# Windowed attention and a squared-ReLU FFN on one core: the first query and key chunks loaded two tokens to a partition and turned by ordinary matmuls, value blocks loaded one by one, and a new hand-written order of the head

## The chip, the cores and the metric

The kernel runs on one core of a Trainium2 chip. The metric is the device time of one execution in microseconds (us). Before the change, three runs gave 879.31, 880.03 and 880.48 us, a median of 880.03 us.

## The reference

The inputs are `q`, `k` and `v` of shape (8 batches, 8 heads, 576 tokens, 64), and the weights `w_in` (512 x 2048) and `w_out` (2048 x 512), all float32. What is computed, in short:

```python
scores = (q @ k.T) / sqrt(64)                  # per batch and head
mask = (0 <= i - j) & (i - j < 64)             # each query sees itself and the 63 keys before it
attn = softmax(where(mask, scores, -1e9))
x = (attn @ v), heads side by side             # 4608 tokens x 512
out = (max(x @ w_in, 0) ** 2) @ w_out          # 4608 x 512
```

## The kernel before, in words

**Tiles.** The 4608 tokens are cut into 12 tiles of 384 tokens (six blocks of 64). For each tile there is an attention part and an FFN part. The attention of a tile comes in three *sections* of four (block, head group) items each. Sections 0 to 2 belong to tile 0 and sections 3 to 5 to tile 1. Tile 1 crosses from batch 0 into batch 1, so sections 4 and 5 need the first 192 tokens of batch 1 as well (`FIRST`, L144).

**FFN.** Each float32 operand is split into a high and a low part, so that a product is three fast matmul passes. `mm1` (L346) makes one 128-wide slice of the hidden layer for a tile (12 matmuls of 384 columns), `evac` (L358) squares and splits it, and `mm2` (L387) accumulates it into the output (9 matmuls of 512 columns). The weights are loaded once, in 16 pieces of 1 MB (`fetch_w`, L77: one DMA for `w_in`, one for `w_out`), and each piece is split by ScalarE and VectorE in six steps (`weight`, L83). Only after all this is in place does the second half of the kernel (L541 on) run as a regular loop over tiles 2 to 11.

**The head, in a written order.** The stretch up to the regular loop has a schedule that is written out by hand: the string `order` (L475) holds one token for each step, and the engines' queues get their instructions in exactly that order. The letters that matter here:

- `L0`.. and `N0`.. load query and key chunks of batch 0 and batch 1 (`load_first`, L151); `v` loads value blocks (`load_v`, L125), `w` a weight piece. All DMAs are issued on SP's queue, in the order of the string.
- `T` and `U` turn a chunk of batch 0 and batch 1, so that the head dimension lies on the partitions (`turn_first`, L161, on TensorE into PSUM), and `t` and `u` copy the turned chunk to SBUF (`copy_first`, L172); the last letter of such a token names the engine (`a` ScalarE, `d` VectorE, `p` GpSimd).
- `S` is a section's score matmuls (L208); `o`, `s`, `z`, `y`, `e`, `f`, `k`, `R`, `m` are the masked softmax (`o` copies the scores out on ScalarE, L216; `s` puts in the masked ones on VectorE, L225 and L226; `e` and `f` are the exponentials, L236); `X` turns the probabilities (L250), `x` masks them on VectorE (L254), `V` multiplies by the values (L272); `H` and `Q` write the result's high and low part (L287, L289).
- `a b c d h l` are the six steps of a weight piece (ScalarE, VectorE three times, ScalarE, VectorE). `M`, `r p g G` and `O` are `mm1`, the evacuation and `mm2`. The first of them, `M0`, needs sections 0 to 2 and the first weight piece; in the string it stands behind section 5's scores and section 3's turn.
- `K5` is five matmuls of the identity with itself whose result nobody reads (`idle`, L497). They fill gaps of TensorE.

A chunk before is 128 tokens, one token a partition, so that one descriptor of the DMA carries the 64 floats (256 bytes) of one token and head. A turn is four PE-mode transposes (L169), one for each of (pair of heads, q or k).

Of the kernel before, what the change touches and what calls it, by code (L numbers as in the profile page):

```python
# [24 lines left out]
def window_attention_relu2_ffn(ctx: ExitStack, tc: tile.TileContext, q, k, v, w_in, w_out, out):  # L25
# [99 lines left out]
    def load_v(b, t):  # L125
        vt = vts[b, t] = att.tile([P, 2, H // 2, D], F32, name="vt", bufs=5)
        for n in range(min(2, NB - 2 * t)):
            s0 = (2 * t + n) * QB
            for m in range(2):
                sp.dma_start(vt[m * QB:(m + 1) * QB, n],  # L130
                             v[b, m * H // 2:(m + 1) * H // 2, s0:s0 + QB, :].rearrange("h s d -> s h d"))
# [11 lines left out]

    FIRST = 2 * TT - S  # L144
    nats, first = {}, {}

    def tokens(b, t):
        return min(P, (FIRST if b else S) - t * P)


    def load_first(b, t):  # L151
        n = tokens(b, t)
        if t % 2 == 0:
            both = wpool.tile([P, 2, 2, H * D], F32, name="w")
            for i in range(2):
                nats[b, t + i] = both[:, i]
        for i, x in enumerate((q, k)):
            sp.dma_start(nats[b, t][:n, i].rearrange("s (h d) -> s h d", d=D),  # L158
                         x[b, :, t * P:t * P + n, :].rearrange("h s d -> s h d"))

    def turn_first(b, t, d):  # L161
        n = tokens(b, t)
        early = b == 0 and 0 < 2 * t + d < 3
        ps = ps_o.tile([P, 2, 2, P], F32, name="oV" if early else "oT", bufs=2 if early else 1)
        if b and (t, d) == (0, 0):
            first[b] = wpool.tile([P, 2, 2, 2, FIRST], F32, name="w")
        for j in range(2):
            for i in range(2):
                pe.transpose(ps[:, j, i, :n], nats[b, t][:n, i, (2 * j + d) * P:(2 * j + d + 1) * P], ident[:n, :n])  # L169
        return ps  # L170

    def copy_first(b, t, d, ps, copy):  # L172
        n = tokens(b, t)
        qk = first[b][:, d] if b else get_turned(b, d)
        copy(qk[:, :, :, t * P:t * P + n].rearrange("p j i s -> p (j i) s"), ps.rearrange("p j i s -> p (j i) s")[:, :, :n])
# [287 lines left out]

    AHEAD, LEAD = 5, 9
    steps = [(t, f) for t in range(2) for f in range(AHEAD)]
    n0 = n1 = AHEAD
    while n1 < NF:
# [8 lines left out]
        L0 L1 w0 L2 T0 v0 T1 t0a t1d S0 w1 T2 o0a T3 K5 t2d v1 s0 t3d a0 z0 S1 L3 y0 b0 f0 N0 T4 K3 c0  # L476
        o1a L4 t4a s1 T5 K5 e0 w2 d0 t5a N1 k0 z1 h0 S2 R0 y1 v2 m0d e1 l0 X0 K6 o2a x0 a1 v3 s2 V0 f1
        b1 H0a k1 T6 K4 w3 z2 R1 y2 t6d m1p v4 f2 Q0 T7 X1 c1 t7a U0 e2 x1 S3 u0a k2 d1 V1 o3a T8 v5 H1a
        R2 s3 m2p t8a T9 a2 Q1 X2 t9d z3 h1 U2 K2 w4 b2 y3 u2a U1 K4 f3 w5 x2 u1a w6 c2 U3 e3 S4 w7 l1
        u3a V2 k3 o4a v6 R3 H2a s4 m3p Q2 S5 a3 z4 X3 o5a b3 M0 y4 f4 x3 e4 c3 V3 r0 k4 d2 p0a M1 v7 H3a  # L480
        g0 R4 Q3 m4p h2 s5 X4 r1 G0 p1a z5 O0 g1 x4 y5 e5 G1 V4 d3 f5 O1 v8 l2 H4a k5 h3 R5 Q4 m5p M2 a4
        l3 w8 w9 X5 r2 b4 a5 M3 w10 x5 p2a w11 g2 c4 r3 V5 w12 p3a G2 g3 w13 d4 O2 w14 G3 h4 H5d O3 w15
        l4 q0 Q5 a6 M4 b5 b6 r4 M5 p4a c5 g4 q1 c6 r5 M6 p5a G4 g5 d6 O4 r6 d5 h6 G5 p6a M7 h5 g6 l5 O5
        r7 G6 a7 l6 p7a O6 b7 g7 a8 G7 M8 c7 b8 O7 r8 p8a d7 g8 M9 G8 h7 c8 O8 r9 l7 p9a g9 d8 a9 M10 G9
        h8 b9 O9 r10 l8 p10a g10 c9 a10 M11 G10 b10 O10 r11 p11a d9 g11 M12 G11 h9 c10 O11 r12 l9 p12a
# [19 lines left out]
    with tc.manual_schedule(engines={E.PE, E.DVE, E.Activation, E.Pool, E.SP}):  # L505
        for token in order.split():
# [4 lines left out]
            elif op == "v":  # L511
                load_v(*divmod(n, (NB + 1) // 2))
# [76 lines left out]
```

## Time and profile before

| | us |
|---|---|
| median of three runs | 880.03 (879.31 to 880.48) |
| the profiled execution's own time | 880.19 |
| its span in the trace | 878.4 |
| TensorE busy | 860.0 of 878.4 (98%) |
| TensorE busy up to the first FFN matmul (0 to 42.59) | 30.55 of 42.59 |
| VectorE busy up to there | 28.45 of 42.59 |

The profiled execution lies 0.16 us above the median, and 1.8 us of it lie outside its span. The page has one number for each engine over the whole run; the head of the kernel, which the change edits, is the first tenth of it. It is best read with the views that take a window of time: the busy times by stretch, the chain of waits that ended last, and the timeline of a single engine. Matmuls with float32 operands appear as two rows of the trace each; transposes as one.

### The profile page before, as it was taken

Reading aid. Unit: us, or ns where it says so; the run is one execution under the profiler, and the core shown is the slowest. Engines: PE = TensorE matmul, PEld = TensorE weight load, DVE = VectorE, ACT = ScalarE, POOL = GpSimd, SP = SyncE. Lnnn points to the kernel's source line nnn. Section 1 sums busy time; section 2 is a strip of 40 time slices with the busy share of each in tenths; the row PEclk is TensorE's granted clock in tenths of the full one; section 3 lists DMA queues with packets and bytes.
Section 4 is the critical chain, followed back from the end, with each engine's and each line's share of the span. In section 5 each row is a group of like instructions: output and inputs, shape, how many; then the busy total and the mean of one; then the engine's idle time right before and its main releaser. Section 6 shows DMA issues by size and latency. Waiting matters only on the chain.

```text
span 878.4 us, 16976 instructions
## 1 busy us (share of the span) xinstructions
PE 860.0 (98%) x6946; PEld 794.7 (90%) x6946; DVE 452.0 (51%) x740; ACT 401.8 (46%) x1147; POOL 50.1 (6%) x70
## 2 busy tenths in 40 slices
PE   6799999999999999999999999999999999999998
PEld 5688998899999999999999999999999999999997
DVE  5799995754455444544455444453445544432222
ACT  5787875644344434434334444334434443432322
POOL 1210000210000000000000000000000000000000
PEclk9899999999999999999999999999999999999999
DMA  9989206460125002421033202141013200100100
GB/s 213 222 270 327 37 4 106 81 155 7 26 55 121 1 1 64 71 48 54 1 55 92 54 2 63 29 81 55 11 21 67 59 1 1 37 1 1 37 1 36
DMA packets 200302, 56.41 MB, mean 64 GB/s; under 512 B 185377, under 2 KB 193569, under 8 KB 200225
## 3 DMA queue, kind: packets, MB, share of 16 engines
q1 hardware_dynamic: 200224, 55.34, 27.4%
q8 instruction: 54, 0.88, 0.4%
q14 instruction: 24, 0.19, 0.1%
HBM read 45.88 MB, written 9.44 MB: 63 GB/s over the span
## 4 chain that ended last, share of the span: by engine, by line
PE 94%; SPq 3%; DMA 1%; ACT 1%; POOL 0%; DVE 0%; issue 0%; POOLq 0%
PE h_ps L352 42%; PE oV L396 26%; PE oT L396 14%; PE s_ps L208 3%; PE v_ps L272 3%; PE s_ps L396 2%; PE v_ps L250 1%; SPq L158 1%; PE v_ps L396 1%; SPq L130 1%; DMA w<-in_k_dram 1%; PE h_ps L500 0%; ACT sel L236 0%; SPq L80 0%; ACT r L361 0%
## 5 line engine op out<-in xcount | busy, mean ns | idle before, releaser
L352 PE MATMUL h_ps<-xhi,w 128*128 128x384 f32 x1536 | 407.0, 327 | 1.9 <-ACT r L361 1.4
L352 PEld LDWEIGHTS h_ps<-xhi,w 128*128 128x128 f32 x1536 | 275.2, 189 | 8.6 <-ACT r L361 3.3
L352 PE MATMUL h_ps<-xlo,w 128*128 128x384 f32 x768 | 250.6, 326 | 0.0
L361 ACT ACTIVATE r<-h_ps 128x384 f32<-128x384 f32 x192 | 93.6, 487 | 286.4 <-PE h_ps L352 285.7
L396 PE MATMUL oV<-w,ghi 128*128 128x512 f32 x704 | 209.5, 379 | 0.0
L366 DVE TENSOR_TENSOR r<-r 128x384 f32<-128x384 f32 x166 | 92.0, 554 | 165.4 <-ACT r L361 165.4
L371 DVE TENSOR_TENSOR glo<-r,ghi 128x384 fp32r<-128x384 f32 x192 | 107.8, 562 | 121.0 <-PE oV L396 82.0
L369 ACT CAST ghi<-r 128x384 fp32r<-128x384 f32 x192 | 98.8, 514 | 117.4 <-DVE r L366 115.4
L396 PEld LDWEIGHTS oV<-w,ghi 128*128 128x128 f32 x704 | 133.2, 189 | 18.8
L352 PEld LDWEIGHTS h_ps<-xlo,w 128*128 128x128 f32 x768 | 145.3, 189 | 4.8
L396 PE MATMUL oV<-w,glo 128*128 128x512 f32 x352 | 133.5, 379 | 0.0
L396 PE MATMUL oT<-w,ghi 128*128 128x512 f32 x352 | 110.2, 395 | 0.0
L236 ACT ACTIVATE sel<-sel,nm 128x64 f32<-128x64 f32 x272 | 90.8, 335 | 17.4 <-DVE nm L230 15.3
L396 PEld LDWEIGHTS oV<-w,glo 128*128 128x128 f32 x352 | 66.6, 189 | 9.4
L245 POOL TENSOR_TENSOR sel<-sel,rs 128x512 f32<-128x512 f32 x33 | 38.4, 1163 | 564.4 <-DVE rs L242 564.4
L396 PE MATMUL oT<-w,glo 128*128 128x512 f32 x176 | 66.8, 379 | 0.0
L254 DVE TENSOR_TENSOR pt<-v_ps,masks 128x1024 f32<-128x1024 f32 x31 | 38.0, 1224 | 46.8 <-PE v_ps L250 46.8
L396 PEld LDWEIGHTS oT<-w,ghi 128*128 128x128 f32 x352 | 59.0, 189 | 2.3 <-issue 0.2
L236 ACT ACTIVATION_READ_ACCUMULATOR sel<-sel,nm 128x1 f32 x272 | 50.9, 187 | 0.0
L140 DVE STREAM_TRANSPOSE qk<-raw 128x1152 f32<-128x1152 f32 x28 | 38.4, 1371 | 1.4 <-issue 1.4
L208 PE MATMUL s_ps<-qk 64*64 64x128 f32 (+1 forms) x1104 | 38.3, 276 | 0.1
L396 PEld LDWEIGHTS oT<-w,glo 128*128 128x128 f32 x176 | 33.3, 189 | 4.7
(80 smaller groups left out, 592.6 us busy)
## 6 DMA issues: line engine op xcount, KB each, us to landing
vt<-in_v_dram SPq DMA_DIRECT2D x144, 64.0 KB, 2.5
out_dram<-osb SPq DMA_DIRECT2D x36, 256.0 KB, 2.3
w<-in_moe_w_in_dram SPq DMA_DIRECT2D x16, 512.0 KB, 6.6
w<-in_moe_w_out_dram SPq DMA_DIRECT2D x16, 512.0 KB, 7.6
raw<-in_q_dram SPq DMA_DIRECT2D x112, 72.0 KB, 2.5
raw<-in_k_dram SPq DMA_DIRECT2D x112, 72.0 KB, 2.5
w<-in_q_dram SPq DMA_DIRECT2D x5, 256.0 KB, 4.6
w<-in_k_dram SPq DMA_DIRECT2D x5, 256.0 KB, 5.2
```

The costliest lines, as they stand in the source:

```text
L140: dve.transpose(get_turned(b, g // 2)[:, g % 2].rearrange("p n t -> p (n t)"), raw.rearrange("p n t -> p (n t)"))
L208: pe.matmul(ps[half * QB:(half + 1) * QB, j, w * P + c0:(w + 1) * P], lhsT=qk[r, 0, qb * QB:(qb + 1) * QB], rhs=qk[r, 1, k0:k0 + P - c0], ...
L236: act.activation(sels[i][:, w, hd], sels[i][:, w, hd], AF.Exp, bias=nms[i][:, n], scale=SCALE, accum_out=sums[i][:, n])
L245: (dve if eng == "d" else pool).tensor_tensor(p, p, rs[i][:, :, None].broadcast_to([P, SW * 2, QB]), ALU.mult)
L254: dve.tensor_tensor(pts[i].rearrange("p (w n) q -> p w n q", n=2), ps_t[i][:, :, None, :].broadcast_to([P, SW, 2, P]), masks.rearrange("p ...
L272: pe.matmul(ps[hd * D:(hd + 1) * D, j, q0:q0 + n * QB], lhsT=vts[b, kb // 2][r, kb % 2, 2 * d + hd, :], rhs=pts[i][r, n0:n0 + n, half * QB ...
L352: pe.matmul(h_ps, lhsT=wparts[f][:, 0, part, kk * P:(kk + 1) * P], rhs=in_turn(xx[:, kk, :]), start=n == 0, stop=n == 3 * NK - 1)
L361: act.activation(by_half(rg[n]), ordered(hs.pop(n)), AF.Relu)
L366: dve.tensor_tensor(rg[n], rg[n], rg[n], ALU.mult)
L369: act.copy(gs[n][0], rg[n])
L371: dve.tensor_tensor(gs[n][1], rg.pop(n), gs[n][0].bitcast(F32), ALU.subtract)
L396: pe.matmul(accs[t][tb], lhsT=gg[:, ts], rhs=in_turn(wparts[f][:, 1, part, :]), start=f == 0 and n == 0, stop=f == NF - 1 and n == 2)
```

## The change

**Chunks.** `load_first` now loads 256 tokens at once, two neighbouring tokens on a partition: a descriptor carries 512 bytes. The last 64 tokens of batch 0 stay one to a partition (256 bytes), and the 192 tokens of batch 1 come as one chunk on 96 partitions.

**Turns.** The even tokens (e = 0) and the odd tokens (e = 1) of a chunk are turned separately, each by eight ordinary matmuls with the identity as the moving operand, 64 output rows at a time. There are as many turns as before (ten for batch 0, four for batch 1), with eight matmuls in place of four transposes. The copy to SBUF writes every second column.

**Values.** `v3` now loads only the first 64-token block of a pair, `i3` the second; before, `v3` loaded both.

**Order.** The string is written anew: fewer fillers in the head (K8, K4, K3 and K5 in place of K5, K3, K5, K6, K4, K2 and K4), the turns `t` nearly all on ScalarE, and VectorE's transposes of the later q and k loads (`D0` to `D7`, L140) at other places, `D0` 124 tokens earlier. The new string begins and then goes on around `N0` and `M0` like this:

```
L0 L1 v0 w0 w1 T0 w2 T1 t0a i0 T2 t1d v1 T3 t2a t3a L2 T4 i1 S0 t4d v2 T5 o0a a0 s0 i2 S1 z0 t5a
...
H2a w7 R3 s4 m3p a3 Q2 S5 i5 z4 X3 o5a b3 M0 v6 y4 f4 i6 x3 e4 c3 V3 r0 k4 d2 p0a M1 v7 H3a g0
```

```diff
-    def load_v(b, t):
-        vt = vts[b, t] = att.tile([P, 2, H // 2, D], F32, name="vt", bufs=5)
-        for n in range(min(2, NB - 2 * t)):
-            s0 = (2 * t + n) * QB
-            for m in range(2):
-                sp.dma_start(vt[m * QB:(m + 1) * QB, n],
-                             v[b, m * H // 2:(m + 1) * H // 2, s0:s0 + QB, :].rearrange("h s d -> s h d"))
+    def load_v(b, t, n):
+        if n == 0:
+            vts[b, t] = att.tile([P, 2, H // 2, D], F32, name="vt", bufs=5)
+        s0 = (2 * t + n) * QB
+        for m in range(2):
+            sp.dma_start(vts[b, t][m * QB:(m + 1) * QB, n],
+                         v[b, m * H // 2:(m + 1) * H // 2, s0:s0 + QB, :].rearrange("h s d -> s h d"))
...
-    def tokens(b, t):
-        return min(P, (FIRST if b else S) - t * P)
+    def chunk(b, t):
+        n = min(2 * P, (FIRST if b else S) - 2 * P * t)
+        return n, 2 if n > QB else 1
...
     def load_first(b, t):
-        n = tokens(b, t)
-        if t % 2 == 0:
-            both = wpool.tile([P, 2, 2, H * D], F32, name="w")
-            for i in range(2):
-                nats[b, t + i] = both[:, i]
+        n, e = chunk(b, t)
+        nats[b, t] = wpool.tile([P, 2, H, 2 * D], F32, name="w")
         for i, x in enumerate((q, k)):
-            sp.dma_start(nats[b, t][:n, i].rearrange("s (h d) -> s h d", d=D),
-                         x[b, :, t * P:t * P + n, :].rearrange("h s d -> s h d"))
+            sp.dma_start(nats[b, t][:n // e, i, :, :e * D],
+                         x[b, :, 2 * P * t:2 * P * t + n, :].rearrange("h (s e) d -> s h (e d)", e=e))
...
         for j in range(2):
             for i in range(2):
-                pe.transpose(ps[:, j, i, :n], nats[b, t][:n, i, (2 * j + d) * P:(2 * j + d + 1) * P], ident[:n, :n])
+                for hd in range(2):
+                    pe.matmul(ps[hd * D:(hd + 1) * D, j, i, :n // m],
+                              lhsT=nats[b, t][:n // m, i, 4 * j + 2 * d + hd, e * D:(e + 1) * D],
+                              rhs=ident[:n // m, :n // m], start=True, stop=True)
...
+        qk = qk.rearrange("p j i s -> p (j i) s")[:, :, 2 * P * t + e:2 * P * t + n:m]
+        copy(qk, ps.rearrange("p j i s -> p (j i) s")[:, :, :n // m])
+
+    def at_once(b, n):
+        return (n // 4, n // 2 % 2, n % 2) if b or n < 8 else (2, n - 8, 0)
```

**What moves on SP.** These are SP's first DMAs before; `DMAHW0` to `DMAHW7` are eight completion semaphores that the DMAs take in turn, so a DMA that waits for one of them waits for the landing of the DMA eight places ahead of it.

```order
L158 DMA w<-in_q_dram 64x8x64 [waits DMAHW6_49]
L158 DMA w<-in_k_dram 64x8x64 [waits DMAHW7_49]
L79 DMA w<-in_moe_w_in_dram 128x4x256 [waits DMAHW0_49]
L80 DMA w<-in_moe_w_out_dram 128x1024 [waits DMAHW1_49]
L158 DMA w<-in_q_dram 64x8x64 [waits DMAHW2_49]
L158 DMA w<-in_k_dram 64x8x64 [waits DMAHW3_49]
L130 DMA vt<-in_v_dram 64x4x64 [waits DMAHW4_49]
```

That is `L4`, the third weight piece `w2`, then `N1` (the last tokens of batch 1), and only then the value blocks of `v2`. After the change the same queue reads, from the third weight piece to the fourth:

```order
L79 DMA w<-in_moe_w_in_dram 128x4x256 [waits DMAHW2_49]
L80 DMA w<-in_moe_w_out_dram 128x1024 [waits DMAHW3_49]
L130 DMA vt<-in_v_dram 64x4x64 [waits DMAHW4_49]
L130 DMA vt<-in_v_dram 64x4x64 [waits DMAHW5_49]
L130 DMA vt<-in_v_dram 64x4x64 [waits DMAHW6_49]
L130 DMA vt<-in_v_dram 64x4x64 [waits DMAHW7_49]
L157 DMA w<-in_q_dram 64x8x64 [waits DMAHW0_49]
L157 DMA w<-in_k_dram 64x8x64 [waits DMAHW1_49]
L130 DMA vt<-in_v_dram 64x4x64 [waits DMAHW2_49]
L130 DMA vt<-in_v_dram 64x4x64 [waits DMAHW3_49]
L130 DMA vt<-in_v_dram 64x4x64 [waits DMAHW4_49]
```

`w2` (the eleventh and twelfth DMA) now stands ahead of `i0`, `v1` and the small chunk `L2`; behind the last row shown come seven more value DMAs and then the two DMAs of `N0`, `v4`, `v5` and `w3`. The tokens of batch 1 therefore stand behind ten value DMAs, eight of which followed them before. The first two of the ten wait for `DMAHW2` and `DMAHW3`, the semaphores of `w2`'s two DMAs. `v5`'s first DMA waits for TensorE too, because its buffer is `v0`'s.

**What moves on TensorE.** Before, the first turns and scores stand like this; `oT` and `oV` are PSUM buffers, one and two of them.

```order
L169 MATMUL oT<-ident,w 128x128 x4
L169 MATMUL oV<-ident,w 128x128 x4
L208 MATMUL s_ps<-qk 64x64 x4
L208 MATMUL s_ps<-qk 64x128 x4
L208 MATMUL s_ps<-qk 64x64 x4
L208 MATMUL s_ps<-qk 64x128 x4
```

After, five turns stand ahead of the same scores (`T0`, then `T1` and `T2`, then `T3` and `T4`):

```order
L170 MATMUL oT<-ident,w 64x128 x8
L170 MATMUL oV<-ident,w 64x128 x16
L170 MATMUL oT<-ident,w 64x128 x16
L216 MATMUL s_ps<-qk 64x64 x4
L216 MATMUL s_ps<-qk 64x128 x4
L216 MATMUL s_ps<-qk 64x64 x4
L216 MATMUL s_ps<-qk 64x128 x4
```

The scores of section 0 need all four turns of the first chunk now, and `T4`, which shares the one `oT` buffer, stands ahead of them too. Further on, before, section 1's product with the values (`V1`) stands ahead of the turns of batch 1's last chunk:

```order
L272 MATMUL v_ps<-w,vt 64x128 x8
L272 MATMUL v_ps<-w,vt 64x64 x16
L169 MATMUL oT<-ident,w 128x64 x8
L250 MATMUL oV<-ident,w 128x128 x4
L169 MATMUL oT<-ident,w 128x64 x4
L500 MATMUL h_ps<-ident 128x128 x2
```

After, the first two turns of batch 1 (`U0` and `U1`, with 96 columns) and a filler stand ahead of `V1`:

```order
L258 MATMUL oV<-ident,sel 128x128 x4
L170 MATMUL oT<-ident,w 64x96 x8
L511 MATMUL h_ps<-ident 128x128 x5
L170 MATMUL oT<-ident,w 64x96 x8
L280 MATMUL v_ps<-w,vt 64x128 x8
L280 MATMUL v_ps<-w,vt 64x64 x16
```

`V1` has moved behind the first batch 1 turns, and so behind the landing of `N0`.

More of the change, by code (lines that the diff above doesn't have):

```diff
@@ L342, in do_load_v @@
             for t in VPARTS[part]:
-                load_v(b, t)
+                for n in range(min(2, NB - 2 * t)):
+                    load_v(b, t, n)
     def mm1(t, f):
@@ L481, in window_attention_relu2_ffn @@
[L481 to L485, printed above, removed]
@@ L495, in window_attention_relu2_ffn @@
+        r27 z7 M28 p27a x6 y7 f7 D4 V6 e7 q6 S8 H6a k7 R7 O24 o8d m7p Q6 s8 X7 g27 G26 O25 r28 z8 x7 y8
+        e8 M29 D5 f8 p28d S9 G27 g28 k8 R8 r29 m8d V7 p29d M30 v11 H7a o9d D6 i11 O26 s9 q7 Q7 z9 X8 g29
+        G28 O27 y9 f9 x8 e9 G29 V8 O28 r30 k9 R9 H8a m9d p30a Q8 g30 M31 G30 D7 X9 r31 O29 p31a x9 g31
+        G31"""
     ps_f = {}
```

51 lines of the change are left out of this document (26 added, 25 removed).

## The prediction

> **What bounds the kernel now.** I read the page first, then the busy times by stretch.
>
> ```profile
> PE 860.0 (98%) x6946; PEld 794.7 (90%) x6946; DVE 452.0 (51%) x740; ACT 401.8 (46%) x1147; POOL 50.1 (6%) x70
> ```
> ```profile
> 0.00:42.59 42.59, 30.55 (x450) 25.63 (x451) 28.45 (x43) 27.48 (x89) 7.99 (x26) 0.92 0.94 214
> 42.59:80.00 37.41, 35.29 (x317) 31.41 (x316) 35.80 (x44) 29.96 (x69) 4.79 (x6) 1.00 0.94 314
> 80.00:870.00 790.00, 789.43 (x6163) 733.91 (x6162) 387.15 (x654) 342.05 (x987) 37.36 (x38) 1.00 0.21 44
> ```
>
> TensorE (the first number behind the stretch's length, then its weight loads, VectorE, ScalarE, GpSimd, granted clock, DMA share, GB/s) is busy 789.43 of 790 us from 80 us on. Nothing can be won there, and what TensorE does there doesn't change. So the run's end is the start of the first FFN matmul, `M0`, at 42.59 us, plus a fixed amount of work, plus the stalls up to 80 us (37.41 - 35.29 = 2.1 us). The change edits what leads to `M0`. The chain of waits tells what did so before:
>
> ```profile
> 25.80 7.25 DMA w<-in_k_dram
> 33.10 0.58 PE oT L169 x3
> ...
> 38.00 1.49 PE s_ps L208 x32
> 39.49 1.10 PE v_ps L272 x46
> ```
>
> The last key tokens of batch 1 land at 33.05 us (25.80 + 7.25), and from there TensorE is the chain: turns, fillers, scores, `V2`. It does that at half speed:
>
> ```profile
> 29.40:32.80 3.40, 1.26 (x10) 0.89 (x9) 2.07 (x5) 1.84 (x4) 1.03 (x2) 1.00 1.30 170
> 32.80:36.20 3.40, 3.20 (x16) 2.99 (x16) 3.37 (x4) 3.00 (x12) 0.00 (x0) 0.50 0.54 121
> ```
> ```profile
> 29.00 0.46 PE L169 MATMUL oT<-ident,w 64*128 64x64 f32 x4
> 30.05 0.46 PE L169 MATMUL oT<-ident,w 64*128 64x64 f32 x4 [0.59 <-ACT qk L175]
> 30.45 0.66 PE L250 MATMUL oV<-ident,w 128*128 128x128 f32 x4
> ```
>
> The granted clock falls to 0.50 right behind a stretch in which TensorE ran only transposes (1.26 us of 3.40).
>
> **When batch 1 lands after the change (L).** First the speed of a 512-byte packet, which the trace doesn't have.
>
> ```profile
> 10.13:41.92 31.79, 24.68 (x393) 21.20 (x395) 26.42 (x40) 24.38 (x85) 5.29 (x11) 0.89 0.96 212
> 2.00:4.00 2.00, 0.00 (x0) 0.00 (x0) 0.00 (x0) 0.06 (x1) 1.44 (x6) 1.00 1.01 227
> 70.00:72.00 2.00, 2.00 (x13) 2.00 (x13) 2.00 (x4) 0.78 (x2) 0.00 (x0) 1.00 1.11 381
> ```
>
> From 2 to 4 us only 256-byte packets of q and k move, at 227 GB/s: 16 x 256 / 227 = 18.0 ns each. From 70 to 72 us only weights move, at 381 GB/s: a piece of 1.049 MB takes 2.75 us, and its 640 packets (512 of 1 KB, 128 of 4 KB, 1638 bytes on average) 69 ns each. A straight line through both gives 27.4 ns for 512 bytes, 299 GB/s. Its bounds are 227 (nothing gained) and 381; I take 299.
>
> The Trainium skill (DMA: Bandwidth & Descriptors, Specifications) gives 512 bytes as the least transfer that reaches line rate. By that the packets would go as fast as the weights; it is a rival below.
>
> ```profile
> 0.79 0.43 SPq L158 DMA_DIRECT2D w<-in_q_dram  x1
> ...
> 15.10 2.59 SPq L130 DMA_DIRECT2D vt<-in_v_dram  x4
> ```
> ```profile
> 4.30 0.45 PE L169 MATMUL oT<-ident,w 128*128 128x128 f32 x1 [4.30 <-DMA w<-in_q_dram]
> ...
> 6.08 1.06 PE L169 MATMUL oV<-ident,w 128*128 128x128 f32 x4
> ...
> 9.32 0.60 PE L169 MATMUL oT<-ident,w 128*128 128x128 f32 x4
> 9.76 1.28 PE L500 MATMUL h_ps<-ident 128*128 128x128 f32 x10
> 11.10 1.16 PE L208 MATMUL s_ps<-qk 64*64 64x128 f32 x32
> ```
> ```profile
> 11.19 1.16 ACT L93 ACTIVATE a<-w 128x1024 f32<-128x1024 f32 x1 [1.69 <-DMA w<-in_moe_w_out_dram]
> ```
>
> Data flow 1.2 us after an issue begins (0.79 to 2.0). The first q (0.26 MB, 1.15 us) has flowed by 3.15 and lets TensorE go at 4.30: 1.15 us from the last byte to the start of work. By the same sums the first weight piece would be usable at 2.0 + 1.05 MB / 227 + 2.75 + 1.15 = 10.5 us; ScalarE gets it at 11.19. Later pieces mix with what stands behind them, so I add 0.6 us. After the change, in SP's order: `L0` and `L1` (2.10 MB at 299) flow until 9.0, `v0` until 9.6, `w0` to `w2` (3 x 2.75) until 17.9; `w2` lands at 17.9 + 1.15 + 0.6 = 19.6. The second DMA of `i1` waits for that landing, and with the eight of `v2`, `i2`, `v3`, `i3` behind it, at 0.65 us each (2.59 / 4; SP is slower here than the transfers), SP reaches `N0` at 19.6 + 9 x 0.65 = 25.5. `N0` flows from 26.7 for 0.786 MB / 299 = 2.6 us, and L = 29.3 + 1.15 = 30.5 us, 2.6 us ahead of before. With 227 GB/s for 512 bytes it would be 33.5, with 381 28.4.
>
> **From L to M0.** `N0` landing releases `U0`; behind it stand K5, `U1` and `V1`, and VectorE waits for `V1` (through `H1`) before `Q1`, and has `b2`, `x2`, `c2`, `R3`, `s4` queued behind `Q1`; `S5`, `X3` and `M0` wait for `s4`. Their prices:
>
> ```profile
> 32.71 0.69 DVE L95 TENSOR_SCALAR a<-a 128x1024 f32<-128x1024 f32 x1 [1.14 <-ACT a L93]
> 33.44 0.69 DVE L96 TENSOR_SCALAR a<-a 128x1024 int32<-128x1024 int32 x1
> 34.05 1.22 DVE L254 TENSOR_TENSOR pt<-oV,masks 128x1024 f32<-128x1024 f32 x1
> 35.18 1.22 DVE L98 SCALAR_TENSOR_TENSOR a<-w,a 128x1024 int32<-128x1024 int32 x1
> 36.31 1.22 DVE L107 TENSOR_TENSOR w<-a,w 128x1024 fp32r<-128x1024 f32 x1
> ...
> 40.17 0.50 DVE L225 COPY_PREDICATED_SCALAR sel<-late,neg 128x256 f32 x1 [1.91 <-ACT sel L216]
> 40.57 0.43 DVE L226 COPY_PREDICATED sel<-late,s_ps 128x256 f32<-128x256 int32 x1
> 41.23 0.69 DVE L289 TENSOR_TENSOR xlo<-v_ps,xhi 128x512 fp32r<-128x512 f32 x1 [0.23 <-ACT xhi L287]
> ```
> ```profile
> 46.42 0.43 PE L352 MATMUL h_ps<-xhi,w 128*128 128x384 f32 x1 [0.27 <-ACT r L361]
> ```
> ```profile
> L175 ACT COPY qk<-oT 128x512 f32<-128x512 f32 x4 | 2.3, 579 | 4.5 <-PE oT L169 4.5
> ```
>
> A turn now is 16 rows (8 matmuls, two rows each). The fillers cost 0.128 us a row (1.28 / 10), the quarter-array score matmuls 0.036 (1.16 / 32), nearly four at a time. Half-array matmuls should go two at a time, 0.064 a row, 1.02 us a turn. Bounds: 0.60, a turn before, and 16 x 0.128 = 2.05, one at a time. With 96 columns I take 0.8. So L to `M0` is rest of `U0` 0.6, K5 1.28, `U1` 0.8, `V1` 1.1, `H1` 0.6, `Q1` 0.7 (41.23), `b2` 1.34 (32.71 to 34.05), `x2` and `c2` 1.13 each, `R3` 0.2, `s4` 0.83 (40.17 to 41.00), and from there to `M0` 1.59 as before (41.00 to 42.59): 11.3 us. By this chain `M0` starts at 30.5 + 11.3 = 41.8.
>
> **The other bound: VectorE.** The scores of section 0 now need four turns and stand behind a fifth. The first keys land at 2.0 + 1.05 MB / 299 + 1.15 = 6.65. Of `T0` to `T3` then 3.75 x 1.02 = 3.8 us are left. Until about 8.9 us TensorE is slow (four transposes cost 1.06 us at 6.08 and 0.60 at 9.32, 1.7 times), which covers 1.3 us of it in 2.25; the rest ends at 11.4. `t3`'s copy (0.58; it writes every second column, for which I take no more, at most double) gives `oT` free, `T4` ends at 13.0, `S0` (1.1) at 14.1, `o0` at 14.8, where `s0` starts; before it was 10.13. VectorE is busy 26.42 of the 31.79 us from there to the end of `Q2` (41.92). After the change the same work stands there but for three copies of turned chunks (`t3`, `t6`, `t9`, 0.6 each by ScalarE's row): 24.6. If VectorE never waits, `Q2` ends at 39.4 + 0.3 for small gaps, and `M0` starts 1.0 later (`s4` ends 0.6 before `Q2`): 40.7 us. The landing decides, by 1.1 us.
>
> **After M0.** `M1` starts at 46.42 before. After, `w3` stands behind `v5`, whose first DMA waits for `V1` (L + 3.8 = 34.3). Two value DMAs and `w3`: landing at 34.3 + 1.3 + 1.2 + 2.75 + 1.15 = 40.7. ScalarE's `a3` (1.16), then `b3`, `x3` (1.34, 1.22) and `V3` (1.1) put `M1` at 45.6, 0.8 us ahead. The gain at `M0` (0.8) is kept.
>
> **The rest of the edits.** Fourteen turns cost about 0.42 us more each (5.9 us), nine fillers fewer save 9 x 0.256 = 2.3; the cover is TensorE's 12.0 us of idle time ahead of `M0` (42.59 - 30.55), and on the chain the dearer `U0` and `U1` are in the sum. `D0` moves into the stretch where VectorE is densest:
>
> ```profile
> 80.00:140.00 60.00, 60.00 (x324) 55.80 (x323) 56.72 (x62) 42.81 (x61) 0.00 (x0) 1.00 0.34 64
> ```
>
> VectorE has 3.3 us of gaps there, and `D0` is 1.4 us. I take 0; if a gap isn't where it is needed it costs up to 1.4. The loads of q and k for `D0` now stand ahead of `w13`; their cover is that `w13` isn't used before the hidden slices of 100 us, else up to 2 us. The split of the value loads adds no DMA. The half clock goes, worth about 3.5 us of TensorE between 33 and 40 us; but what stood in its shade was VectorE, so the gain is already inside the sums above.
>
> The sum: 880.19 - 0.8 = 879.4 for the profiled execution, which lies 0.16 above the median: **879.2 us**, 0.1% faster. A measurement of this kernel can tell about 0.2% (1.8 us) from no change, so this is "no difference that shows".
>
> **Rivals.**
> - *Turns one at a time (slower).* At 2.05 us a turn, `T0` to `T4` leave 9.7 us at 6.65, end with the copy's wait at about 17.9, and `s0` starts at 19.6. VectorE's floor then is 19.6 + 24.6 + 0.3 + 1.0 = 45.5: 2.9 us late, 882.9. It decides from 1.8 us a turn (s0 at 18.4) on. For it: nothing in the trace is a half-array matmul. Against it: the quarter-array ones overlap. Chance 0.12.
> - *The clock falls again (slower).* If L is past 32.4, TensorE has only `X1`, four transposes, for about 3.4 us, as at 29.4 to 32.8 before. Half clock on the 3.9 us from `U0` to `V1` and on later pieces costs 2 to 3.5 us on top of L + 11.3 = 43.7 and more: 882.5 to 884. Chance 0.08. The Trainium skill (TensorE: Matmul & The Clock Gate, Part 4) says that transpose mode doesn't count as TensorE being busy; the trace agrees (1.26 us of transposes, then 0.50). By that rule the new turns, being ordinary matmuls, guard the clock, and only the wait for `N0` is open.
> - *512 bytes at the weights' rate (faster).* With 381 GB/s L is 28.4 and the chain gives 39.7; the first keys land at 5.9, `s0` at 14.2, and VectorE's floor is 40.1: 2.5 us ahead, 877.5. Turns near 0.6 us give much the same from the other side. For it: SP's order puts nothing else in the way. Against it: 256-byte packets show a cost per packet of 8.6 ns on that line. Chance 0.27, with milder mixes of both.
>
> **How the numbers follow.** Forecast (within 0.2%) 0.53, faster 0.27, slower 0.12 + 0.08 = 0.20. The range reaches from just under the faster rival, 877.2, to 882.6, a little short of the slower two, and leaves out about 2 in 10.
>
> **What would show it.** Right: `U0` waits for `N0` and goes near 30.5 us, `M0` near 41.8, no stretch at half clock behind 9 us, VectorE's wait for `H1` ahead of `Q1` is about 1 us. A turn's eight matmuls near 1.0 us at full clock. Wrong: `M0` outside 40 to 44, `s0` past 17, a clock of 0.50 again, or new waits of TensorE between 50 and 140 us.

## The result, and the profile after

The changed kernel takes **889.24 us** (888.24 to 890.00, four runs) against 879.67 us (877.61 to 880.48, four runs) of the kernel before on the same chip: a ratio of **1.0117**, 95% interval 1.0099 to 1.0134. It is 1.2% slower, where no difference was forecast, and lies outside the range. The profiled execution took 888.24 us, its span is 886.5. All ratios here are of executions in the chip's ordinary state, which leaves out one of run b2's twelve (1007.86 us).

First the busy times by stretch: up to `M0`, up to 80 us, and the rest (TensorE's busy time stands behind the length, then weight loads, VectorE, ScalarE, GpSimd, granted clock, DMA share, GB/s).

```profile
0.00:48.92 48.92, 34.53 (x600) 29.70 (x601) 26.93 (x39) 27.64 (x91) 10.69 (x27) 0.93 0.71 191
48.92:80.00 31.08, 27.55 (x277) 24.20 (x276) 29.14 (x37) 24.57 (x62) 2.45 (x4) 1.00 0.98 313
80.00:870.00 790.00, 789.37 (x6161) 733.34 (x6160) 393.68 (x662) 344.75 (x991) 33.89 (x35) 1.00 0.22 46
```

`M0` starts at 48.92 us in place of 42.59: 6.3 of the 8.1 us by which the span grew. Behind `M0` 837.6 us follow in place of 835.8; of these 1.8 us, 1.4 are stalls up to 80 us (31.08 - 27.55 = 3.5, before 2.1). From 80 us on nothing changed (789.37 of 790). The frame of the prediction holds, then: the loss is in the head.

The chain of waits shows what leads to `M0` now (start, duration, what):

```profile
10.59 10.71 DMA w<-in_moe_w_out_dram
21.32 0.60 SPq L130
...
24.60 1.29 SPq L130
...
27.25 0.61 SPq L130
27.86 0.04 issue
27.91 0.60 SPq L157
28.51 0.04 issue
28.56 6.27 DMA w<-in_k_dram
34.82 0.04 issue
34.87 1.23 PE oT L170 x12
36.10 2.43 PE h_ps L511 x10
38.53 1.44 PE oT L170 x16
39.97 1.11 PE v_ps L280 x48
```

Read from the top: `w2` lands; SP, which had waited for it, issues nine value DMAs one after the other (eight at 0.60 to 0.62 us, one at 1.29); then `N0`; 6.3 us later its keys are there; then TensorE needs 2.43 us for ten rows of the trace with fillers (the idle matmuls of a `K` token) that took 1.28 us at full clock in the kernel before. The clock stands in the windows around it:

```profile
25.00:30.00 5.00, 4.14 (x111) 3.71 (x105) 4.86 (x8) 4.79 (x22) 0.87 (x2) 1.00 0.38 87
30.00:35.00 5.00, 1.88 (x15) 1.22 (x16) 5.00 (x7) 3.39 (x12) 0.61 (x1) 0.80 0.81 173
35.00:40.00 5.00, 5.00 (x42) 4.37 (x46) 1.28 (x3) 1.81 (x9) 1.51 (x3) 0.52 0.00 0
```

TensorE does 1.88 us of work in five, the clock falls to 0.52, and in the last stretch the DMA engines do **nothing**. Why, SP's timeline and its waits say: `v5` waits for `V1`, and all weights from `w3` on are queued behind it.

```profile
29.13 13.10 SPq L130 DMA_DIRECT2D vt<-in_v_dram  x4
42.27 0.60 SPq L79 DMA_DIRECT2D w<-in_moe_w_in_dram  x1
```
```profile
SPq L130 <- PE v_ps L280: 10.9, 2, 10.6
```

So `w3` is issued at 42.27, and ScalarE's `a3` (48.52), VectorE's `x3` and TensorE's `V3` come late behind it, with `M1` at 53.57 (46.42 before):

```profile
48.52 1.35 ACT L93 ACTIVATE a<-w 128x1024 f32<-128x1024 f32 x1 [1.51 <-DMA w<-in_moe_w_out_dram]
```
```profile
52.51 1.13 PE L280 MATMUL v_ps<-w,vt 64*64 64x128 f32 x48 [1.39 <-DVE w L262]
53.57 0.43 PE L361 MATMUL h_ps<-xhi,w 128*128 128x384 f32 x1
```

At the other end of the head, the first turns and the first masked scores (`s0`):

```profile
8.12 3.63 PE L170 MATMUL oV<-ident,w 128*64 128x128 f32 x32
11.53 1.51 PE L170 MATMUL oT<-ident,w 128*64 128x128 f32 x16
13.75 1.10 PE L170 MATMUL oT<-ident,w 128*64 128x128 f32 x16 [0.71 <-ACT qk L179]
```
```profile
16.44 0.50 DVE L233 COPY_PREDICATED_SCALAR sel<-late,neg 128x256 f32 x1 [0.85 <-ACT sel L224]
```

A turn of 16 rows takes 1.10 us from 13.75 us on, as foreseen, but the first four are slow until about 12.5 us (32 rows in 3.63 us), and VectorE starts on `s0` at 16.44 (10.13 before).

### The profile page after: what moved, and what is told of

Read it like the earlier page. It is cut to its first block, busy times and chain, and to the rows that moved or that the text cites. A ratio compares the mean times of both kernels' runs of the same rounds, so it can differ in the third digit from the quotient of the medians.

```text
span 886.5 us, 17253 instructions
## 1 busy us (share of the span) xinstructions
PE 864.1 (97%) x7096; PEld 798.5 (90%) x7096; DVE 452.7 (51%) x741; ACT 401.2 (45%) x1150; POOL 47.0 (5%) x66
## 4 chain that ended last, share of the span: by engine, by line
PE 86%; DVE 4%; DMA 4%; SPq 2%; ACT 1%; issue 1%; DVEq 0%
PE h_ps L361 39%; PE oV L405 25%; PE oT L405 13%; PE s_ps L216 3%; PE v_ps L280 3%; DMA w<-in_moe_w_out_dram 3%; DMA w<-in_k_dram 2%; PE v_ps L258 1%; DVE a L98 1%; DVE w L107 1%; SPq L130 1%; PE s_ps L405 1%; ACT a L93 1%; DVE glo L380 1%; DVE a L100 1%
## 5 line engine op out<-in xcount | busy, mean ns | idle before, releaser
L253 POOL TENSOR_TENSOR sel<-sel,rs 128x512 f32<-128x512 f32 x29 | 34.1, 1175 | 566.8 <-DVE rs L250 566.8
L140 DVE STREAM_TRANSPOSE qk<-raw 128x1152 f32<-128x1152 f32 x28 | 38.4, 1373 | 3.6 <-DMA raw<-in_k_dram 1.9
```

The lines of the kernel that those rows point to most:

```text
L140: dve.transpose(get_turned(b, g // 2)[:, g % 2].rearrange("p n t -> p (n t)"), raw.rearrange("p n t -> p (n t)"))
L253: (dve if eng == "d" else pool).tensor_tensor(p, p, rs[i][:, :, None].broadcast_to([P, SW * 2, QB]), ALU.mult)
```

## The experiments

Each edit below moves tokens of the order string, against the changed kernel in the runs e and h, against the kernel before in the runs b and m1 and m2; m3 and m4 mix both forms.

**Theory:** the order of SP's queue costs the time: (a) `N0` behind ten value DMAs behind `w2`, (b) the half clock that follows from the long wait, (c) `v5`'s wait for `V1` in front of the weights. **Rival A:** the two-token form itself costs it, by its dearer turns and by the start of VectorE's work 6 us later. **Rival B:** the order behind `M1` costs it. "Behind M0" is the span less the start of `M0`; both come from one profiled execution of each kernel, while the ratio is of the medians, to the kernel before on the same chip.

| run | s0 | M0 | behind M0 | ratio (95% interval) |
|---|---|---|---|---|
| before, first profile | 10.13 | 42.59 | 835.8 | 1 |
| before, second profile (b0) | 10.52 | 39.01 | 836.6 | 1 |
| after | 16.44 | 48.92 | 837.6 | 1.0117 (1.0099 to 1.0134) |
| e4 fillers ahead of `U0` | 16.23 | 46.43 | 837.7 | 1.0092 (1.0073 to 1.0110) |
| e2 `v5` behind `w7` | 16.42 | 49.50 | 836.0 | 1.0091 (1.0074 to 1.0108) |
| e1 `N0` behind `w2` | 16.41 | 46.67 | 837.8 | 1.0076 (1.0061 to 1.0091) |
| e3 both | 15.64 | 48.13 | 836.0 | 1.0063 (1.0044 to 1.0082) |
| h1 old order, new loads | 14.95 | 48.04 | 835.7 | 1.0049 (1.0032 to 1.0066) |
| e8 `L2`, `N0` ahead of `w2`, `v5` behind `w7` | 16.20 | 43.38 | 837.6 | 1.0045 (1.0029 to 1.0061) |
| e9 e8 with `T4` behind `S0` | 15.44 | 42.62 | 836.4 | 1.0033 (1.0019 to 1.0046) |
| e10 e9 with `v5` behind `w4` | 15.18 | 42.92 | 836.1 | 1.0014 (1.0002 to 1.0025) |
| e11 e10 with fillers ahead of `T0` | 13.28 | 44.58 | 835.7 | 1.0040 (1.0027 to 1.0052) |
| e12 e11 with `i0` behind `v0` | 13.30 | 43.74 | 836.4 | 1.0033 (1.0017 to 1.0049) |
| m1 old kernel, `N1` late | 10.52 | 45.00 | 835.8 | 1.0048 (1.0033 to 1.0064) |
| m2 old kernel, `S0` delayed | 13.20 | 40.76 | 836.9 | 1.0019 (1.0008 to 1.0030) |
| b1 old kernel, `N1` ahead of `w2` | 10.12 | 43.91 | 835.6 | 1.0027 (1.0014 to 1.0041) |
| b2 old kernel, fillers ahead of `U2` | 10.47 | 41.56 | 835.7 | 1.0026 (1.0013 to 1.0040) |
| b3 b2 with fillers ahead of `T0` | 9.61 | 40.75 | 837.5 | 1.0014 (1.0001 to 1.0026) |
| m3 mixed | 10.57 | 43.08 | 835.7 | 1.0014 (1.0002 to 1.0025) |
| m4 mixed, `L2` ahead of `w0`, `t6` on ScalarE | 10.44 | 47.35 | 835.6 | 1.0071 (1.0052 to 1.0089) |

### The half clock alone (e4)

```diff
-f2 U0 K5
+f2 K12 U0 K5
```

> The changed kernel with twelve more matmuls of the identity (K12) ahead of U0, in the stretch where TensorE waits for N0; nothing else moves. Theory (the half clock costs about 2.4 us of M0's delay on top of the late landing): the granted clock stays at 1.00 from 30 to 40 us, U0 to V1 takes 3.9 us in place of 6.2, V1 ends near 38.8 in place of 41.03, M0 near 46.7 in place of 48.92, w3 lands 2 us earlier; time 886.5 to 887.5 us. Rival (the clock there is covered by other waits): M0 and time as in the changed kernel, 889.

Measured: 886.57 us, `M0` at 46.43. The windows of this run:

```profile
30.00:35.00 5.00, 4.33 (x44) 3.85 (x44) 5.00 (x7) 3.14 (x11) 0.61 (x1) 1.00 0.87 181
35.00:40.00 5.00, 4.40 (x102) 3.79 (x96) 1.82 (x5) 3.54 (x13) 1.52 (x3) 1.00 0.02 6
```

The clock stays at 1.00, and `M0` comes 2.5 us earlier, with the keys landing where they did (first used at 34.64 us, 34.87 before). Part (b) is shown, with its price in the profiled executions; in the medians it is 2.2 us by the ratios. The weights stay late: 837.7 us behind `M0`.

### v5 behind the weights (e2), N0 ahead of the values (e1), both (e3)

```diff
-U2 v5 H1a
+U2 H1a
...
-w7 R3
+w7 v5 R3
```
```diff
-T0 w2 T1
+T0 w2 N0 T1
...
-f0 N0 d0
+f0 d0
```

> The changed kernel with one token moved: v5, whose buffer waits for V1, stands behind w7 in SP's queue instead of ahead of w3. Theory: M0 stays near 48.9 us with the half clock ahead of it, but w3 lands by about 36 us, a3 no longer waits, M1 comes 3.8 us behind M0 (52.7), and the late weights between 60 and 80 us go; time about 885 us (883.5 to 886.5), 3 to 5 us less than the changed kernel. Rival A (the turns ahead of S0): 889, no change. Rival B (order behind M1, other than the weights' lateness): 888 to 889.

> The changed kernel with one token moved: N0 (queries and keys of batch 1) stands directly behind w2 in SP's queue, ahead of the ten value DMAs. Theory (SP's order costs the time: N0 behind the values, then the half clock, then w3 behind v5's wait for V1): the keys land about 3 to 4 us behind w2's 21.35 us, near 25 us in place of 34.87; no half clock between 30 and 40 us; V1 ends by 35 in place of 41.03, so v5's wait ends earlier and w3 lands near 41 in place of 48.46; M0 near 42.5 to 43.5 (VectorE's own work from s0 on), M1 near 47; time about 881 us (880 to 883). Rival A (the new turns ahead of S0, which start VectorE 6 us later, cost the time): M0 stays above 46, time 886 or more. Rival B (the order behind M1 costs it): M0 comes early, but the time stays above 885.

> Both moves at once: N0 behind w2, v5 behind w7. Theory: M0 near 42.5 to 43.5, M1 3.8 us behind it, no late weights; time 878.5 to 880.5 us, no slower than the kernel before. Rival A: above 885. Rival B: above 884.

e2 did what (c) says: `M0` no earlier, and 1.6 us less behind it. The time fell by less than expected, 2.3 us by the ratios. e1 missed: 885.92 us, `M0` at 46.67 instead of 43, which is where Rival A had put it. TensorE's waits and the clock in e1 show another reason than Rival A's:

```profile
26.59 0.33 PE L170 MATMUL oT<-ident,w 64*64 64x64 f32 x4 [1.57 <-DMA w<-in_q_dram]
27.54 0.56 PE L170 MATMUL oT<-ident,w 64*64 64x64 f32 x12 [0.62 <-DMA w<-in_k_dram]
```
```profile
30.00:32.00 2.00, 2.00 (x52) 2.00 (x50) 1.80 (x4) 1.42 (x2) 0.78 (x2) 0.50 0.46 104
```

These are `T8`'s matmuls on `L2` (64 partitions): `N0` had taken its place, `L2` was now late, and the half clock came there. e3 has both effects and 884.71 us, at least 4 us more than the theory gave; it has the same wait for `L2` (3.06 us) and 6.83 us of half clock.

### No landing in the way (e8, e9, e10)

```diff
-w1 T0 w2
+w1 L2 N0 T0 w2
...
-w7 R3
+w7 v5 R3
```

with `L2`, `N0` and `v5` gone from their old places, and for e9 `T4` and `t4d` behind `S0`, for e10 `v5` behind `w4` instead of `w7`.

> The changed kernel with three tokens moved in SP's queue: L2 and N0 stand ahead of w2 and of the ten values, and v5 stands behind w7. In the run with N0 alone moved, TensorE then waited 2.2 us for L2 and the half clock came there. Theory (the landings and the clock are the whole loss, VectorE's work from s0 on the next bound): no DMA wait of TensorE between 20 and 40 us and no half clock; s0 near 16, then 25.4 us of VectorE's work, 0.5 us of gaps and 1.0 us to M0: M0 near 43; with 836 us behind M0 as in the run with both moved, a span of 879 and a time of 880 to 882 us. Rival A (S0 comes 6 us later than in the kernel before, and the head is a chain of waits that moves as a whole): M0 at 46 or later, time 884 us or more.

> As the run with keys first, and T4 with its copy stands behind S0 instead of ahead of it. Theory: s0 starts about 1 us earlier (near 15), M0 near 42, time 879 to 881 us, about 1 us less than with T4 ahead. Rival A: M0 follows s0 in the same way, but from 46: 45, time 883 or more. If TensorE's order there decides nothing, both have the same time.

> As the run with keys first and T4 late, but v5 stands behind w4 instead of behind w7 (there TensorE waited 0.8 us for v5's values at 52 us, 2.0 us in the run before that). Theory: M0 stays at 42.6, no wait for values behind M1, 835.7 to 836.0 us behind M0 in place of 836.4; time 0.4 to 1 us less, 0.1% to 0.3% over the kernel before. Rival A: unchanged.

From e8, VectorE's first masked scores, `M0`, and a later wait of TensorE:

```profile
16.20 0.50 DVE L233 COPY_PREDICATED_SCALAR sel<-late,neg 128x256 f32 x1 [0.85 <-ACT sel L224]
```
```profile
43.38 0.41 PE L361 MATMUL h_ps<-xhi,w 128*128 128x384 f32 x1
54.36 0.87 PE L280 MATMUL v_ps<-pt,vt 64*64 64x64 f32 x32 [1.97 <-DMA vt<-in_v_dram]
```

`M0` stands where VectorE's work from `s0` puts it: expected near 43, found 43.38, and with `s0` 0.76 us earlier in e9 exactly 0.76 us earlier (42.62). The times, 882.56 and 881.95 us, lie 0.6 and 1 us above the ranges expected. In e8 and e9 `v5` was late in its turn (1.97 us, 0.83 in e9); behind `w4` it isn't, and e10 is at 1.0014. From e10:

```profile
15.18 0.50 DVE L233 COPY_PREDICATED_SCALAR sel<-late,neg 128x256 f32 x1
```
```profile
42.92 0.41 PE L361 MATMUL h_ps<-xhi,w 128*128 128x384 f32 x1
```

Loads, turns and Rival B's later order are the same in e10 as in the changed kernel: **moving five tokens takes back 1.03 of the 1.17%** in the medians. Rival B falls with that, for 836.1 us follow `M0`, as in the kernel before. Rival A doesn't fall altogether, as the granted clocks of the kernel before will show.

### The same faults put into the kernel before (m1, m2)

```diff
-t5a N1 k0
+t5a k0
...
-v3 s2
+v3 N1 s2
```

> The kernel before with one token moved: N1 (the last tokens of batch 1) stands behind the values of v2 and v3 in SP's queue, as the changed kernel has N0 behind its values; nothing else changes. Theory: the keys land 4 to 6 us later (33 to about 38), the half clock comes ahead of them, M0 near 46 to 48, time 3 to 6 us over the kernel before (ratio 1.0035 to 1.007). Rival A (the new loads and turns are what costs, the place of the keys in SP's queue doesn't): time within 1 us of before.

In m1 the keys come 2.4 us later than in the first profile of before, behind a long wait at half clock:

```profile
34.67 0.33 PE L169 MATMUL oT<-ident,w 64*128 64x64 f32 x1 [4.11 <-DMA w<-in_q_dram]
35.50 0.58 PE L169 MATMUL oT<-ident,w 64*128 64x64 f32 x3 [0.50 <-DMA w<-in_k_dram]
```

and the old kernel, with its old loads and turns, loses 0.48%. So (a) and (b) need nothing of the two-token form. `M0`, at 45.00, lies under the 46 to 48 expected, since the keys were to come 4 to 6 us later.

> The kernel before (one-token loads, transposes, old order) with fourteen matmuls of the identity (K14) ahead of S0, so that the first scores and s0 come 4 to 5 us later (10.13 to about 15) and nothing else changes. Theory (the landing of batch 1's keys at 33 us and VectorE's throughput decide, so a late start is caught up): VectorE's floor is 15 + 26.4 + 0.3 + 1.0 = 42.7, M0 between 42.6 and 43.5, time 879.5 to 881 us. Rival A (the late start itself costs the time): M0 near 46 to 47, time 883 to 884.5 us.

m2 (K14 ahead of `S0`) put `s0` at 13.20, 3 us late, and still has `M0` at 40.76:

```profile
13.20 0.50 DVE L225 COPY_PREDICATED_SCALAR sel<-late,neg 128x256 f32 x1
```
```profile
40.76 0.41 PE L352 MATMUL h_ps<-xhi,w 128*128 128x384 f32 x1
```

That is earlier than 42.59, and the 880.27 us are in the theory's range; yet they are 0.19% **over** the kernel before, whose median on that chip was 878.62. Neither theory had that, and it asked for a second profile of the kernel before.

### The kernel before once more (b0), and its clock (b1, b2, b3)

> The kernel before, unchanged, for a profile of its head on the chip of the three runs beside it. Both theories: s0 near 10.1, M0 between 41 and 43, keys of batch 1 near 33 us.

```profile
31.87 0.40 PE L169 MATMUL oT<-ident,w 64*128 64x64 f32 x3 [0.92 <-DMA w<-in_k_dram]
...
39.01 0.41 PE L352 MATMUL h_ps<-xhi,w 128*128 128x384 f32 x1
```

This execution took 877.33 us: keys at 31.87 in place of 33.10, no half clock, `M0` at 39.01. The runs of the kernel before that stand beside the experiments lie between 876.73 and 882.28 us, and the profile on which the prediction was built (880.19) is in the upper half of that. Against 39.01, a late `s0` does cost: 2.7 us of it in m2 are 1.75 us at `M0`.

The mean granted clock on record for each execution says how usual b0 is. One stretch of half clock in the head, 3.41 us long, takes the mean of a run from 1.000 to 0.998, two take it to 0.996 (as in the two first profiles). Of the 87 executions of the kernel before that stand beside the experiments, three are at 0.999 or 1.000 (876.73 to 876.77 us), 37 at 0.998 (mean 878.6) and 47 below (mean 880.1). So the kernel before nearly always runs a part of its head at half clock and is then 2 to 3 us longer, while e10 keeps the full clock in all ten executions (0.999 or 1.000, 880.30 to 881.54 us). Compared at full clock, with those three or with b0, e10 is still about 4 us slower, with `M0` 3.9 us later than in b0 and `s0` 4.7 us later: the 0.14% is a lasting loss of that size, less about 3 us that the kept clock goes with. The changed kernel itself (0.993 to 0.996) is 8 to 10 us slower than the kernel before at 0.996 (mean 880.0).

Three tries to have `M0` this early each time:

> The kernel before with two tokens moved in SP's queue: the second load of batch 1 (N1) and then w2 stand directly behind L4, so the keys of batch 1 come ahead of w2; loads, turns and the rest of the order are the old ones. Theory (the place of the keys in SP's queue decides the head, not the two-token form): the keys land by 28 us in place of 33.05, no half clock, M0 near VectorE's floor of 10.1 + 26.4 + 1.3 = 37.9, so 38 to 41; time 1 to 3.5 us under the kernel before. Rival (the landing is covered, M0 is set elsewhere): M0 near 42.6, time as before, 0 to 0.5 us off. Rival (the gain is given back at a3, which waits for w3): M0 early, M1 near 45.5, time within 1 us of before.

> The kernel before with eight more matmuls of the identity (K8) ahead of U2, where TensorE waits for N1; nothing else. Two profiles of the kernel before differ there: in one the clock falls to 0.50 and M0 starts at 42.59, in the other it stays at 1.00 and M0 starts at 39.01. Theory: the half clock is all of that difference, so that with fillers M0 is near 39 to 40 each time; time 1 to 2.5 us under the median of the kernel before (ratio 0.997 to 0.999). Rival (M0 differs by when N1 lands): ratio 0.9995 to 1.0015.

> As the run with fillers ahead of U2 in the kernel before, and eight matmuls of the identity ahead of T0 as well, while TensorE waits for the first queries. Theory: the first turns and scores are not slow (four transposes took 1.06 us at 6.08 and 0.60 at 9.32), s0 starts about 1 us earlier than 10.1, M0 near 38 to 39; time up to 1 us under the run without them. Rival (VectorE isn't what sets M0 there): same time as the run without them.

All three missed, at 1.0027, 1.0026 and 1.0014. In b1 `w2`, moved back, was late: VectorE and TensorE wait behind `a2`, and the half clock follows that wait.

```profile
35.43 0.69 DVE L95 TENSOR_SCALAR a<-a 128x1024 f32<-128x1024 f32 x1 [2.68 <-ACT a L93]
```
```profile
36.66 1.12 PE L169 MATMUL oT<-ident,w 128*128 128x128 f32 x4 [3.34 <-ACT w L175]
```

In b2 the fillers hold the clock at `U2`, but in its profile it falls earlier, where TensorE waits for `N0`:

```profile
24.00:28.00 4.00, 3.79 (x19) 3.55 (x19) 2.60 (x4) 2.05 (x10) 1.13 (x2) 0.60 1.09 197
```

b3 has the same stretch (0.57). The clock goes with the time of the kernel before, as the 87 executions show, but whether the half clock alone separates its two profiles is not settled; the keys landed 1.2 us apart too.

### Old order with the new loads, and both forms mixed (h1, m3, m4)

> The changed kernel's two-token loads and its turns by matmuls, but in the old order of the head as far as it goes: the chunk of 256 tokens stands where its two halves stood, N0 where N1 stood (ahead of the values of v2 and v3), T0 to T3 ahead of S0, T4 to T7 ahead of S2, and the rest of the string (fillers, weights, D0 to D7) as in the kernel before. Theory (loads and turns are near neutral, the order of SP's queue is what costs): keys of batch 1 land between 28 and 32 us, M0 between 41 and 44, time 878.5 to 881.5 us. Rival A (the turns or the two-token loads themselves cost it): M0 above 46, time 885 or more.

> Mixed: the first 256 tokens of batch 0 come in two one-token chunks and are turned by transposes as in the kernel before, so that S0 needs two turns only; the other tokens come by two a partition and are turned by matmuls; L3 (the last 64 tokens) and N0 stand ahead of w2, most values and v5 behind it; the rest as in the old order. Theory: s0 near 10.5, keys of batch 1 near 20 us, no half clock, M0 38 to 41, time 1 to 3.5 us under the kernel before. Rival A (two-token loads and turns by matmuls cost by themselves): M0 above 43, time over before.

> The mixed kernel (first 256 tokens one-token with transposes, the rest by two a partition) with L2 ahead of w0 in SP's queue and t6's copy on ScalarE; in the mixed run VectorE had waits of 2.42 us at 20.1 and 1.22 us at 24.0 behind T4 to T7, which waited for L2's keys until 14.93. Theory: T4 runs by 12.5, the two waits shrink to 1 us together, M0 near 40 to 41 in place of 43.08; time 1.5 to 2.5 us less, ratio 0.9985 to 1.0000. Rival (the dearer turns of T4 to T7 set it): M0 stays above 42, ratio 1.001 to 1.002.

h1 missed its `M0` (48.04). In its profile four turns stand ahead of `S0` and two more ahead of `S2`, the probabilities of section 1 come later, and TensorE waits 1.88 us for them and falls to half clock:

```profile
32.19 1.00 PE L258 MATMUL oV<-ident,sel 128*128 128x128 f32 x4 [1.88 <-POOL sel L253]
```

Three of h1's five executions kept the clock at 1.000, though, and took 882.58 to 883.09 us, so the half clock isn't what costs h1 its time. In an order that wasn't made for them the new loads and turns cost 0.49%: Rival A's `M0` came in the profile, its time (885) not quite. m3 keeps the early `s0` (10.57), but VectorE then waits behind `T4` to `T7`, and it is no better than e10:

```profile
20.08 0.69 DVE L185 COPY qk<-oT 128x512 f32<-128x512 f32 x1 [2.42 <-PE oT L176]
...
23.95 1.23 DVE L268 TENSOR_TENSOR pt<-oV,masks 128x1024 f32<-128x1024 f32 x1 [1.22 <-PE oV L264]
```

m4, meant to mend that, moved `w0` back and waited for it instead (ScalarE's `a0`, and VectorE behind it, 3.07 us at 15.50):

```profile
15.50 0.69 DVE L95 TENSOR_SCALAR a<-a 128x1024 f32<-128x1024 f32 x1 [3.07 <-ACT a L93]
```

### Warm first turns in the best order (e11, e12)

```diff
-T0 w2
+K10 T0 w2
```

> The best order of the changed kernel so far (L2 and N0 ahead of w2, T4 behind S0, v5 behind w4) with ten matmuls of the identity (K10) ahead of T0. Theory: what is left of its loss is VectorE's late start (s0 15.2 against 10.1), of which the slow first turns are a part (32 rows took 3.3 us at 8.06, 16 rows 1.04 at 11.18): with warm turns s0 starts near 13.7, M0 near 41.2, time 1 to 1.5 us less, ratio 0.9990 to 1.0005. Rival A (the loads set s0): s0 stays at 15, ratio 1.0014 as without the fillers.

> As the run with the changed kernel's best order and ten matmuls of the identity ahead of T0, but the values i0 (tokens 64 to 127) stand right behind v0 in SP's queue; in the run without that, s0 came at 13.28 and TensorE then waited 2.35 us at 28.3 for i0's values, with the half clock behind it. Theory (SP's order again: whichever transfer stands behind w2 is late): no wait for values, no half clock, s0 near 13.5, M0 near 41 to 41.5, 835.7 to 836.2 us behind it; time 1 to 1.5 us under the order with cold turns (ratio 0.9990 to 1.0008 to the kernel before). Rival A (the two-token loads and turns cost by themselves): ratio 1.0014 or more.

`s0` came to 13.28, near the 13.7 expected, and the time got worse. In e11 TensorE meets `i0`'s values, which stand behind `w2`; in e12, with `i0` moved forward, VectorE meets `w0`, which that moved back:

```profile
28.32 0.56 PE L280 MATMUL v_ps<-pt,vt 64*64 64x64 f32 x14 [2.35 <-DMA vt<-in_v_dram]
```
```profile
17.17 0.69 DVE L95 TENSOR_SCALAR a<-a 128x1024 f32<-128x1024 f32 x1 [2.32 <-ACT a L93]
```

In both profiles the half clock came right behind the wait. No version was faster than the kernel before. That e10's remaining loss is the late `s0`, the second half of Rival A, is argued, not shown: in executions at full clock the kernel before takes 876.7 to 877.3 us with `s0` at 10.5 (b0), m2 879.6 (mean of six at 1.000) with 13.2, and e10 880.8 (mean of ten) with 15.2; but e11 and e12, which were to show it, ran into other waits first.

## Why the prediction was wrong, point by point

- **The frame** (only the head matters; `M0` plus a fixed remainder) held: 835.6 to 837.8 us behind `M0` in every profile.
- **The 512-byte packets** held: first keys used at 6.78 us (6.65 foreseen). **A turn** held: 1.10 us once the first four were over (1.02).
- **The landing of batch 1 is the step that failed**: L = 30.5 was forecast, bounds 28.4 to 33.5, and 34.87 measured. Term by term: `w2` landed 1.7 us later (21.32, not 19.6). From there SP took 6.6 us for the nine value DMAs, where nine at 0.65 were counted: 0.7 more, all of it in the one that held SP for 1.29 us, so that it was at `N0` at 27.9, not 25.5. And `N0` took 7.0 us from its issue to the use of its keys, not 5.0, the largest of the three: it was given 299 GB/s from 1.2 us after its issue, and the DMA engines moved 108 GB/s from 29 to 30 us, then 337, 237, 222 and 53 in the four microseconds behind. By the sizes of the packets most of that is `N0`'s own until 32 us, and `v4`'s values stand behind it; so why `N0` flowed so slowly stays open. Each term was a little short, all in the same direction, and the upper bound varied the packet rate alone.
- **"The clock falls again" was a rival at 0.08; it came true.** Its condition (L past 32.4) and its price (2 to 3.5 us) were right: e4 measures 2.5 us at `M0`. Its time (882.5 to 884) was still 5 us short, since L lay 2.5 us past the condition and `w3` came late. The chance was wrong because it hung on L. That transposes rather than idleness let the clock fall before is not shown: in the stretch read for it TensorE was also idle for 2.1 of 3.4 us. The first profile of before had 6.83 us of half clock too, the changed kernel's has as much: the forecast counted on its going, and it stayed.
- **From L to `M0`**: 11.3 us forecast, 14.05 measured with the half clock, and 11.8 in e4 (46.43 - 34.64, its keys' first use). This sum was right.
- **VectorE's floor**: `s0` at 14.8 forecast, 16.44 measured. TensorE's first turns were taken to be slow until 8.9 us; they were until 12.5 (32 rows in 3.63 us at 8.12). From `s0` to `M0` 25.9 us were forecast, and e8 and e9 measure 27.18. The rule was right, its two terms 1.6 and 1.3 short. With the landings out of the way this floor alone sets `M0` at 43.38 (e8): even a right L would have left `M0` some 1.6 us behind the 41.8 forecast.
- **"w3 lands at 40.7, M1 0.8 us ahead"**: the wait of `v5` for `V1` was seen and priced, but with L = 30.5. With the true L and the half clock `V1` ended at 41.03 instead of 34.3, `w3` was issued at 42.27, and `M1` came 7.2 us later than in the kernel before. The sum gave this step one value, with no thought for what it does at an L past its bound; that is the 1.6 us which e2 takes back.
- **`D0` and the loads ahead of `w13`** at nothing: TensorE's idle time from 80 to 140 us is 0.48 us (none before). Right within its bound.
- **The base**: the profile of before had a half clock and `M0` at 42.59, b0 has 39.01. By its time and its clock (0.996) the first is an ordinary execution, and b0 a rare one. But the 41.8 forecast for `M0`, a gain of 0.8 us on the first, would have been a loss of 2.8 on b0: a part of the gain hoped for was the half clock of the kernel before, and not its order.
- Of the other rivals, *turns one at a time* fell (1.10 us a turn), and *512 bytes at the weights' rate* too: while `L0` and `L1` flow, the DMA engines move 334 and 323 GB/s (3 to 5 us) and then 289 to 291 (6 to 9 us), not 381. The Trainium skill (DMA: Bandwidth & Descriptors, Specifications), which gives 512 bytes as enough for line rate, isn't borne out here.

Where the faster loads went, the last column of the windows of after shows:

```profile
0.00:10.00 10.00, 3.91 (x34) 3.54 (x36) 0.06 (x1) 1.90 (x2) 2.70 (x15) 1.00 0.90 225
10.00:20.00 10.00, 8.61 (x150) 7.44 (x147) 4.84 (x8) 4.66 (x13) 0.53 (x1) 1.00 1.11 346
20.00:30.00 10.00, 8.41 (x173) 7.39 (x172) 9.34 (x13) 9.79 (x36) 3.24 (x4) 1.00 0.49 96
30.00:40.00 10.00, 6.88 (x55) 5.58 (x58) 6.28 (x9) 5.20 (x21) 2.13 (x4) 0.66 0.41 87
```

By 20 us it had moved 5.7 MB, and before 4.3 (215 GB/s in both halves). By 40 us it was 7.5 MB, and before 8.8 (243 and 204 GB/s): the lead was lost while SP issued values, and then waited.

## What to carry to other kernels

When one queue issues all transfers in order, price an order by the landing of the last transfer ahead of the one that matters, add up the issue of each one behind it, and give every landing a range of its own that allows for a slower flow than the one seen elsewhere. Look for an issue that waits for a compute engine: everything queued behind it, here all weights, gets the delay of that engine. And take two or more profiles of the kernel before when its times spread over 0.5%, since the one at hand may show a stall that others don't have; and compare executions at the same granted clock, since a variant that keeps the clock can look as good as a kernel that loses it.

## What the runs showed of the hardware

- The half clock lasts 6.83 us in the changed kernel (from 33.0), 3.41 in e1, b2 and h1, 10.24 in m1: two, one and three times 3.41 us in the records of the granted clock. The Trainium skill (TensorE: Matmul & The Clock Gate, Part 1) gives a free-running window of 3413 ns; the trace agrees. It fits with this that the same kernel has the half clock in one execution and not in another.
- The waits ahead of a half clock need not be long: 1.88 us in h1, 1.00 and 0.76 us around 23 us in b2.
- A 64 KB value DMA mostly holds SP for 0.61 us, about as long as a 512 KB half of a weight piece (0.34 to 0.74 up to 11 us), and sometimes longer (1.29 us at 24.60; 2.82 at 18.10). Nine of them in a row were 6.6 us of SP, and from 25 to 30 us the DMA engines moved 87 GB/s.
- The half-array matmuls of a turn take 0.069 us a row (1.10 / 16) against 0.128 for the full-array filler, as two side by side would.
